# First-layer chunks beside the attention: six tiles of 256 tokens become four of 384, with the instruction order planned anew

## The chip, the cores and the metric

The kernel runs on one core of a Trainium2 chip. The metric is device time in microseconds (us) for one execution. All work is in fp32: a matrix product is either a full fp32 product or three products of rounded parts in fp32r ("high times high, high times low, low times high").

## What is computed

Causal attention over 4 batches of 8 heads, 576 positions and head width 64 (2304 tokens in all), then a gated feed-forward layer on the RMS-normalised result, then a second feed-forward layer.

```python
scores = q @ k.T / 8 + min(-(cum[i] - cum[j]), 0), causal    # cum = cumsum(max(s, 0))
x = softmax(scores) @ v                                      # heads side by side: 2304 x 512
xn = x / sqrt(mean(x * x) + 1e-6) * rms_g
x = (silu(xn @ w_gate) * (xn @ w_val)) @ w_out               # 512 -> 1536 -> 512
h = x @ w_in                                                 # 512 -> 2048
out = (h * sigmoid(1.702 * h)) @ w_out2                      # 2048 -> 512
```

## The kernel before

The program has two stages on TensorE. The first, some 250 us, is the attention, head after head; the second is a chain of products for the two feed-forward layers (`tmul`, with `chain=True`), which keeps a fixed order among its own instructions.

A head goes through these steps. `prep` loads its queries and keys. Heads 0 to 13 (`QF`) multiply in full fp32 and read the loaded tiles (slot s3, `QS` and `KS`, shown as `s_0_136`, and `KX`/`QX` in slot sc). Heads 14 to 31 are split: the pair of heads is loaded into the same slot s3, rounded and subtracted, and 12 copies from SBUF to SBUF lay the parts out as `QA`, `KA` (slot s2) and `QB`, `KB` (slot s1); their score products are fp32r. Where the first stage turns from the one form to the other, the split heads can be loaded only when the last full fp32 scores have read slot s3. I call this place the handover. `scores` is followed on VectorE by the row minimum, on ScalarE by `expo`, on GpSimd by `norm`; `transp` transposes the weights on TensorE (bank 2 and 3, copied out by ScalarE or VectorE), and for two heads together `pv` multiplies them with the values in two pieces. After 8 heads a batch is whole: `rms` sums squares on TensorE, twelve small VectorE instructions take the root, two short groups of transposes spread it (`ident,small` in the rows; bank 4, shown as `b_70`), and VectorE scales the batch's columns of `xT`, first 320 of them, then 256.

The gated layer is cut into twelve chunks of 128 of its 1536 columns. The first two (`G0`) are computed for tokens 0 to 1535 already in the first stage, beside the attention, in `fa_tile`: `TIN` cuts these tokens into tiles. I call this work the filler. Each tile is split into rounded parts (`XH`, slot sc, `sc` in the rows), multiplied with gate and value weights (`gv`: 3 matmuls to a planner's unit, 8 units to a chunk), passed through tanh and two VectorE products (`TH`, slot se), split again (`FH`, slot sd, `sd` in the rows) and multiplied with the output weights (`outp`); the product is copied to `YO` and written to DRAM (`y_d`). Before the change gate and value of a tile share bank 6 (`b_72`), 256 columns each, and the output products use bank 7 (`b_73`).

Slots are pieces of SBUF that one set of tiles after another uses. Slot sd holds `FH` until the filler ends and then `B21`, a block of the chain's left operand, so `B21` is written only after the last output product of the filler.

The order of all instructions is made by a planner in the kernel: `op` records each instruction with an estimated cost, `plan` lists them by readiness and due time, and the program then holds every engine to that order. Costs and due times are numbers in `PRM`: `HD` (due times of head pairs), `FD` (start and end of the due times of a tile's filler), `WD` (weights), `TA` (where the chain's ideal times begin), `PVC` (cost of the two pieces of `pv`), `INNER` (a factor on the cost of copies inside SBUF). A unit, recorded by one call of `op`, is never split by the planner.

Of the kernel before, what the change touches and what calls it, by code (L numbers as in the profile page):

```python
# [15 lines left out]
AF = mybir.ActivationFunctionType  # L16
ALU = mybir.AluOpType
# [7 lines left out]
PRM = {  # L25
    "G0": 2, "NWS": 18, "NWO": 6,
    "QF": set(range(14)),
    "TIN": [(t * 256, 256) for t in range(6)],
    "PPB": 5, "PTB": 12, "XHB": 7, "HHB": 5,
    "VIRT": 311296,  # L30
    "SLOTS": {
# [5 lines left out]
    },  # L37
# [8 lines left out]
    "TA": 260.97, "REB": 3, "EARLY": False, "MAG": "AV", "PASS": 0, "ISSUE": 0.6, "INNER": 1.5, "IDLE": 3, "PEN": {}, "PVC": (1.0, 2.25),  # L46
}


# [1 line left out]
def attention_then_swiglu_then_gelu(ctx: ExitStack, tc, qT, kT, vp, s, w1, w2, gT, out):  # L51
# [3 lines left out]
    P = 128  # L55
    KT = DM // P
# [3 lines left out]
    G0 = PRM["G0"]  # L60
    QF = PRM["QF"]
    TIN = PRM["TIN"]
    TS = max(n for _, n in TIN)
    TA = sum(n for _, n in TIN)
# [16 lines left out]
    PB = [pq.tile([P, 512], F32, tag=f"b{i}", name=f"b{i}") for i in range(8)]  # L81
# [17 lines left out]
    def few(n):  # L99
# [7 lines left out]

    SHAPE = {
        "Q": [S], "K": [S], "mask": [S], "SQ": [S], "VS": [5, 2 * D], "SR": [S], "ZR": [S], "CH": [S], "CL": [S], "PA": [1920], "PT": [512],
        "XH": [2, TS], "TH": [TS], "FH": [2, TS], "YO": [2, TS], "w": [2, 512], "wb": [512], "ws": [512],  # L110
        "MK": [2, 2, H2], "HH": [2, H2], "M5": [H2], "SG": [H2], "V1": [H2], "RE": [H2], **{nm: [2, 2, H2] for nm in NAMES},
    }
    ROUND = ("CH", "CL", "QA", "QB", "KA", "KB", "XH", "FH", "w", "HH", *NAMES)
# [45 lines left out]
    def get(name, n=None):  # L159
        if n is None:  # L160
            return BUF[name][0]
        return [BUF[f"{name}{i}"][0] for i in range(n)]

    QS, KS, QB, KB, QA, KA, VS, TH = (get(x, 2) for x in ("QS", "KS", "QB", "KB", "QA", "KA", "VS", "TH"))
    def wide(name, n):
        t = get(name)
        return virtual[:, t.offset:t.offset + n * S]

    mask, SQ, SQT, YO = (get(x) for x in ("mask", "SQ", "SQT", "YO"))
    PA = get("PA", NB)  # L170
    XH, FH = get("XH", PRM["XHB"]), get("FH", PRM["HHB"])
    PT = get("PT", PRM["PTB"])
# [200 lines left out]
    def tt(o_, x, y, o, eng="VG", **kw):  # L373
        op(eng, lambda e: e.tensor_tensor(out=o_, in0=x, in1=y, op=o), **kw)
# [16 lines left out]
    def dma(o_, i_, eng="S", **kw):  # L391
        op(eng, lambda e: e.dma_start(out=o_, in_=i_), dma=True, **kw)
# [38 lines left out]
    def mm3(e, o, w, wc, x, first, last):  # L431
        for n, (i, j) in enumerate(((0, 0), (0, 1), (1, 0))):
            e.matmul(o, w[:, i, wc:wc + P], x(j), start=first and n == 0, stop=last and n == 2)
# [1 line left out]


    hd = {}
    pt_i, xh_i, fh_i, th_i = [0], [0], [0], [0]

    def turn(bufs, i):  # L440
        i[0] += 1
        return bufs[(i[0] - 1) % len(bufs)]
# [92 lines left out]
    def scores(h, u):  # L535
        ps = bank(h, "s", 5 * h + u)
        blks = {0: [(1, 0, 0, 192), (0, 192, 0, 64)], 1: [(2, 0, 0, 320)], 2: [(3, 0, 0, 448)],
                3: [(4, 0, 0, 288)], 4: [(4, 0, 288, 288)]}[u]
        i = h % 2

        def fn(e):
            for qb, c0, k0, n in blks:
                q0 = Q0[qb]
                o = ps[:, c0:c0 + n]
                if h in QF:
                    kt, qt = kq_of(h)
                    e.matmul(o, qt[0:HB + 64, q0:q0 + P], kt[0:HB + 64, k0:k0 + n], start=True, stop=True)
                else:
                    e.matmul(o, QA[i][:, q0:q0 + P], KA[i][:, k0:k0 + n], start=True, stop=False)
                    e.matmul(o, QB[i][:, q0:q0 + P], KB[i][:, k0:k0 + n], start=False, stop=True)  # L550

        first_score.append(op("T", fn)["i"])
        mx = MX[h % NB]
        for qb, c0, k0, n in blks:
            pt = p_of(h, qb)
            moff = S - QK[qb] + k0 if qb else S - P
            col = 5 if k0 else qb

            def fn(e, qb=qb, c0=c0, k0=k0, n=n, pt=pt, moff=moff, col=col):
                e.tensor_tensor_reduce(  # L560
                    out=pt[:, k0:k0 + n], in0=ps[:, c0:c0 + n], in1=mask[:, moff:moff + n],
                    scale=-0.125, scalar=mx[:, 4:5] if k0 else BIG, op0=ALU.add, op1=ALU.min,
                    accum_out=mx[:, col:col + 1])

            op("V", fn)
            if qb != 4 or k0:
                expo(h, qb)
# [146 lines left out]
    def fa_tile(j, due):  # L714
        t0, n = TIN[j]
        xh = []
        for k in range(KT):
            x = xT[:, k, t0:t0 + n]
            t = turn(XH, xh_i)
            rnd("AV", t[:, 0, :n], x)  # L720
            sub(t[:, 1, :n], x, t[:, 0, :n])
            xh.append(t)
        hs = []
        steps = []

        def gv(c, u, k):
            if u == 0 and k == 0:
                fs["g"] = fs.get("g", -1) + 1
            ps = PB[PRM["BANK"]["g"][fs["g"] % len(PRM["BANK"]["g"])]].rearrange("p (u n) -> p u n", u=2)
            op("T", lambda e: mm3(e, ps[:, u, :n], WS[3 * c + u], k * P, lambda i: xh[k][:, i, :n], k == 0, k == KT - 1),  # L730
               **due())
            if u == 1 and k == KT - 1:
                th = turn(TH, th_i)[:, :n]
                hh = turn(FH, fh_i)
                hs.append(hh)
                g, v = ps[:, 0, :n], ps[:, 1, :n]
                op("A", lambda e: e.activation(out=th, in_=g, func=AF.Tanh, scale=0.5))
                op("V", lambda e: e.scalar_tensor_tensor(out=th, in0=th, scalar=1.0, in1=g, op0=ALU.add, op1=ALU.mult))
                tt(th, th, v, ALU.mult, eng="V")
                rnd("AG", hh[:, 0, :n], th)  # L740
                sub(hh[:, 1, :n], th, hh[:, 0, :n])

        def outp(c, o):
            half, i = divmod(o, 2)
            ps = PB[PRM["BANK"]["o"][0]].rearrange("p (u n) -> p u n", u=2)
            hh, w = hs[c], WS[3 * c + 2]

            def fn(e):
                for q, (x, y) in enumerate(((0, 0), (0, 1), (1, 0))):
                    e.matmul(ps[:, i, :n], w[:, x, o * P:o * P + P], hh[:, y, :n],  # L750
                             start=c == 0 and q == 0 and i == 0, stop=c == G0 - 1 and q == 2 and i == 1)

            op("T", fn, **due())
            if c == G0 - 1 and i == 1:
                def cpy(e):
                    if e.tag == "A":
                        e.activation(out=YO[:, :, :n], in_=ps[:, :, :n], func=AF.Copy, scale=0.5)
                    else:
                        e.tensor_scalar(out=YO[:, :, :n], in0=ps[:, :, :n], scalar1=0.5, scalar2=1.0, op0=ALU.mult, op1=ALU.mult)

                op("AV", cpy)
                dma(y_d[:, 2 * half:2 * half + 2, t0:t0 + n], YO[:, :, :n])

        for c in range(G0):
            for u in range(2):
                for k in range(KT):
                    gv(c, u, k)
            if c:
                for o in range(2):
                    outp(c - 1, o)  # L770
        for o in range(2):
            outp(G0 - 1, o)
        for c in range(G0):
            for o in (2, 3):
                outp(c, o)

    fill_n = [0]
    per = G0 * (2 * KT + KT)

    def fill_due():  # L780
        j, i = divmod(fill_n[0], per)
# [690 lines left out]
```

## Time and profile before

| | us |
|---|---|
| median of 3 runs (1001.4 to 1001.81) | 1001.64 |
| the profiled execution | 1002.01 |
| its span, first to last instruction | 1000.2 |
| TensorE busy in that span | 990.4 |
| VectorE, ScalarE, GpSimd busy | 655.0, 563.0, 286.1 |

The span is what the trace covers; 1.8 us of the profiled execution lie around it. A matmul counts as busy from its start to the modelled end of its pipeline, so that neighbours overlap; how long TensorE needs for one of a row of equal matmuls is read from the distance between starts instead.

### The profile page before, as it was taken

The page shows a single profiled execution, that of the slowest core. Times are in us where ns is not written, and L with a number is a line of the kernel's source. Part 1 is how long each engine was busy: PE and PEld are TensorE (multiplying, and loading weights), DVE is VectorE, ACT ScalarE, POOL GpSimd, SP SyncE. Part 2 cuts the span into 40 slices and gives each one's busy share as a digit, 9 for nine tenths or more (in the row PEclk, how much of TensorE's full clock was granted, in tenths as well). Part 3 has the DMA queues.
Part 4 walks back from the last instruction along what each step waited for, and adds up shares of the span by engine and source line. Part 5 has one row for each costly group of instructions (what it writes and reads, how often), then busy time and mean ns, then how long its engine had stood idle before and what let it go on. Part 6 is the DMA issues. An engine that isn't in the chain of part 4 may idle for free.

```text
span 1000.2 us, 16551 instructions
## 1 busy us (share of the span) xinstructions
PE 990.4 (99%) x5882; PEld 910.7 (91%) x5882; DVE 655.0 (65%) x1532; ACT 563.0 (56%) x1298; POOL 286.1 (29%) x388
## 2 busy tenths in 40 slices
PE   9999999999999999999999999999999999999998
PEld 6777888898999999999999999999889998899987
DVE  8777886777878888546766858874653564353323
ACT  8988786786576555334544436776644463353322
POOL 5666653554332133102322303332320231020000
PEclk9999999999999999999999999999999999999999
DMA  5247766853775762661583676653375045505541
GB/s 181 91 126 183 211 176 177 205 140 118 278 256 225 281 240 98 242 221 43 170 317 144 241 287 231 273 205 123 108 281 221 29 161 232 189 1 197 207 165 63
DMA packets 63050, 183.51 MB, mean 183 GB/s; under 512 B 7028, under 2 KB 23924, under 8 KB 62968
## 3 DMA queue, kind: packets, MB, share of 16 engines
q1 hardware_dynamic: 62968, 182.46, 53.1%
q8 instruction: 46, 0.75, 0.3%
q14 instruction: 36, 0.29, 0.1%
HBM read 122.32 MB, written 44.19 MB: 166 GB/s over the span
## 4 chain that ended last, share of the span: by engine, by line
PE 89%; DVE 4%; ACT 2%; DMA 2%; issue 1%; SPq 1%; POOL 0%; DVEq 0%; ACTq 0%
PE b L208 89%; DVE s L208 1%; ACT s L208 1%; DVE xT L208 1%; SPq L208 1%; DMA s<-in_kT_dram 1%; DMA s<-in_qT_dram 1%; DMA y_d<-sc 0%; DVE b L208 0%; DVE sf L208 0%; POOL wa L208 0%; DVE sc L208 0%; DMA s<-s 0%; ACT st L208 0%; ACT si L208 0%
## 5 line engine op out<-in xcount | busy, mean ns | idle before, releaser
L208 ACT ACTIVATE s<-b 128x384 f32<-128x384 f32 (+1 forms) x267 | 127.6, 489 | 146.4 <-PE b L208 81.2
L208 DVE TENSOR_TENSOR xT<-b,xT 128x384 f32<-128x384 f32 (+1 forms) x158 | 92.6, 599 | 88.7 <-PE b L208 88.0
L208 ACT ACTIVATE b<-b 128x384 f32<-128x384 f32 x125 | 58.2, 478 | 107.8 <-DVE b L208 72.0
L208 POOL TENSOR_TENSOR wa<-wa,st 128x512 int32<-128x512 int32 x50 | 65.9, 1319 | 171.7 <-DVE wa L208 79.0
L208 DVE TENSOR_TENSOR s<-b,s 128x384 fp32r<-128x384 f32 (+1 forms) x121 | 66.4, 553 | 67.3 <-ACT s L208 62.7
L208 PE MATMUL b<-s,w 128*128 128x384 f32 x540 | 107.4, 336 | 0.5 <-DVE s L208 0.3
L208 PE MATMUL b<-s 128*128 128x288 f32 (+11 forms) x420 | 99.2, 361 | 1.8 <-DVE small L208 1.4
L208 PEld LDWEIGHTS b<-s,w 128*128 128x128 f32 x540 | 94.9, 188 | 2.1 <-DVE s L208 1.4
L208 POOL TENSOR_SCALAR wm<-wm 128x512 f32<-128x512 f32 x68 | 41.8, 615 | 140.4 <-ACT wm L208 41.9
L208 PEld LDWEIGHTS b<-s 128*128 128x128 f32 (+1 forms) x420 | 66.9, 192 | 14.8 <-issue 6.3
L208 DVE TENSOR_TENSOR b<-b,s 128x384 f32<-128x384 f32 x82 | 46.1, 562 | 51.6 <-PE b L208 41.4
L208 PE MATMUL b<-sc,w 128*128 128x256 f32 (+1 forms) x396 | 67.3, 304 | 0.0
L208 POOL TENSOR_SCALAR s<-s,small 128x192 f32<-128x192 f32 (+4 forms) x100 | 52.2, 542 | 33.1 <-DVE small L208 11.9
L208 ACT ACTIVATE s<-s,small 128x448 f32<-128x448 f32 (+4 forms) x100 | 55.1, 551 | 9.8 <-DVE small L208 9.6
L208 ACT ACTIVATE st<-st 128x512 int32<-128x512 uint32 x68 | 45.6, 673 | 22.3 <-DMA st<-in_w_dram 22.1
L208 PEld LDWEIGHTS b<-sc,w 128*128 128x128 f32 x396 | 57.1, 189 | 1.0 <-DVE se L208 0.2
L208 PE MATMUL b<-sd,w 128*128 128x384 f32 (+1 forms) x312 | 56.3, 313 | 0.3 <-ACT se L208 0.3
L208 PE MATMUL b<-s,s 128*128 128x384 f32 (+1 forms) x252 | 54.9, 346 | 0.0
L208 PE MATMUL b<-w,s 128*128 128x512 f32 x189 | 51.1, 391 | 0.0
L208 PE MATMUL b<-s,sk 128*128 128x384 f32 x246 | 50.8, 335 | 0.2 <-DVE s L208 0.2
L208 DVE CUSTOM_DVE_ANT_0 s<-b,s 128x288 f32<-128x288 f32 (+4 forms) x100 | 39.3, 424 | 15.7 <-PE b L208 15.5
L208 PEld LDWEIGHTS b<-sd,w 128*128 128x128 f32 x312 | 49.1, 189 | 0.5 <-ACT se L208 0.5
(267 smaller groups left out, 2390.6 us busy)
## 6 DMA issues: line engine op xcount, KB each, us to landing
st<-in_w_dram SPq DMA_DIRECT2D x68, 512.0 KB
s<-s SPq DMA_DIRECT2D x108, 144.0 KB
xT<-y_d SPq DMA_DIRECT2D x3, 1536.0 KB
s<-pc11B SPq DMA_DIRECT2D x6, 768.0 KB
s<-pc21B SPq DMA_DIRECT2D x6, 768.0 KB
out_dram<-xT SPq DMA_DIRECT2D x18, 256.0 KB
s<-in_vp_dram SPq DMA_DIRECT2D x16, 256.0 KB
y_d<-se SPq DMA_DIRECT2D x12, 256.0 KB
```

Of the source, the lines that this page charges most:

```text
L208: return lambda *args, **kw: f(*[real(x) for x in args], **{k: real(x) for k, x in kw.items()})
```

## The change

The filler's tiles are 384 tokens wide, four in place of six, over the same 1536 tokens. A tile's gate has bank 6 to itself and its value bank 7. The tanh of a chunk and the first VectorE product are recorded behind the last gate unit instead of behind the last value unit. An output product of both chunks is one unit of 6 matmuls (before: two units of 3, in banks shared by two outputs); the four of a tile alternate between banks 6 and 7, each is copied out alone (128x384 in place of 128x512), and each is written to DRAM by a DMA of its own, 16 DMAs in place of 12. There are four `XH` buffers for the four of a tile (before 7), three of `FH` (5), one `TH` (2), and two of `YO`. The scores of each head get due times (`SD`), all other due times are new, `TA` goes from 260.97 to 257.35, `INNER` from 1.5 to 1.0, and `PVC` from (1.0, 2.25) to (0.81, 2.22). So the planner puts out another order, in the first stage above all.

```diff
-    "TIN": [(t * 256, 256) for t in range(6)],
-    "PPB": 5, "PTB": 12, "XHB": 7, "HHB": 5,
+    "TIN": [(t * 384, 384) for t in range(4)],
+    "PPB": 5, "PTB": 12, "XHB": 4, "HHB": 3,
...
-    "TA": 260.97, "REB": 3, "EARLY": False, "MAG": "AV", "PASS": 0, "ISSUE": 0.6, "INNER": 1.5, "IDLE": 3, "PEN": {}, "PVC": (1.0, 2.25),
+    "TA": 257.35, "REB": 3, "EARLY": False, "MAG": "AV", "PASS": 0, "ISSUE": 0.6, "INNER": 1.0, "IDLE": 3, "PEN": {}, "PVC": (0.81, 2.22),
...
-        first_score.append(op("T", fn)["i"])
+        sd = PRM["SD"][h]
+        first_score.append(op("T", fn, due=sd if sd < 690 else None, g=f"s{h}")["i"])
...
         def gv(c, u, k):
-            if u == 0 and k == 0:
-                fs["g"] = fs.get("g", -1) + 1
-            ps = PB[PRM["BANK"]["g"][fs["g"] % len(PRM["BANK"]["g"])]].rearrange("p (u n) -> p u n", u=2)
-            op("T", lambda e: mm3(e, ps[:, u, :n], WS[3 * c + u], k * P, lambda i: xh[k][:, i, :n], k == 0, k == KT - 1),
+            ps = PB[PRM["BANK"]["go"[u]][0]]
+            op("T", lambda e: mm3(e, ps[:, :n], WS[3 * c + u], k * P, lambda i: xh[k][:, i, :n], k == 0, k == KT - 1),
                **due())
+            if u == 0 and k == KT - 1:
+                fs["th"] = turn(TH, th_i)[:, :n]
+                th = fs["th"]
+                op("A", lambda e: e.activation(out=th, in_=ps[:, :n], func=AF.Tanh, scale=0.5))
+                op("V", lambda e: e.scalar_tensor_tensor(out=th, in0=th, scalar=1.0, in1=ps[:, :n], op0=ALU.add, op1=ALU.mult))
...
-        def outp(c, o):
-            half, i = divmod(o, 2)
-            ps = PB[PRM["BANK"]["o"][0]].rearrange("p (u n) -> p u n", u=2)
-            hh, w = hs[c], WS[3 * c + 2]
+        def outp(o):
+            ps = PB[PRM["BANK"]["go"[o % 2]][0]][:, :n]
 
             def fn(e):
-                for q, (x, y) in enumerate(((0, 0), (0, 1), (1, 0))):
-                    e.matmul(ps[:, i, :n], w[:, x, o * P:o * P + P], hh[:, y, :n],
-                             start=c == 0 and q == 0 and i == 0, stop=c == G0 - 1 and q == 2 and i == 1)
+                for c in range(G0):
+                    for q, (x, y) in enumerate(((0, 0), (0, 1), (1, 0))):
+                        e.matmul(ps, WS[3 * c + 2][:, x, o * P:o * P + P], hs[c][:, y, :n],
+                                 start=c == 0 and q == 0, stop=c == G0 - 1 and q == 2)
...
-    per = G0 * (2 * KT + KT)
+    per = G0 * 2 * KT + KT
```

Over the whole program TensorE gets 288 filler matmuls of 384 columns for 432 of 256 columns; nothing else is taken off it or added to it. In the order before these 432 stand in 59 runs between other work, in the new order the 288 stand in 39.

The first place is TensorE's order at the handover (`s_0_136`: full fp32 scores; `s_0_885` and `s_0_231`, now `s_0_928` and `s_0_234`: the tiles of split heads; `64x...` rows: `pv`). Between the last full fp32 score and the first split one stand, before, 41 transposes, two groups of three for the root, and one first piece of `pv`. These are the last rows of it:

```order
L208 MATMUL b_69<-ident,s_0_159 128x128 x3
L208 MATMUL b_68<-ident,s_0_165 128x128 x4
L208 MATMUL b_69<-ident,s_0_165 128x128 x4
L208 MATMUL b_70<-sb_397,s_0_149 64x256
L208 MATMUL b_70<-sf_289,s_0_149 64x256
L208 MATMUL b_70<-sb_397,s_0_149 64x128
L208 MATMUL b_70<-sf_289,s_0_149 64x128
L208 MATMUL b_67<-s_0_885 128x192
```

And now:

```order
L211 MATMUL b_68<-ident,s_0_165 128x128 x4
L211 MATMUL b_72<-sc_915,w_125 128x384 x3
L211 MATMUL b_69<-ident,s_0_165 128x128 x4
L211 MATMUL b_68<-ident,s_0_165 128x128 x4
L211 MATMUL b_72<-sc_915,w_125 128x384 x3
L211 MATMUL b_70<-sg_309,s_0_149 64x256
L211 MATMUL b_70<-sb_377,s_0_149 64x256
L211 MATMUL b_70<-sg_309,s_0_149 64x128
L211 MATMUL b_70<-sb_377,s_0_149 64x128
L211 MATMUL b_69<-ident,s_0_165 128x128 x3
L211 MATMUL b_68<-ident,s_0_131 128x128 x4
L211 MATMUL b_67<-s_0_928 128x192
```

What moved: the groups for the root went ahead of the last full fp32 score, a first and a second piece of `pv` came in behind it, and six filler matmuls with one more first piece stand ahead of the split score. In all the stretch now holds 37 transposes, two first pieces and one second piece of `pv`, and 6 filler matmuls.

The second place is TensorE's order where the filler ends and the chain takes over (`sd_1363`, now `sd_1339`: the filler's output products; `sd_3073`, now `sd_2903`: block `B21`; `sg` and `sf`: blocks of the last batch's tokens). Before:

```order
L208 MATMUL b_70<-ident,small 128x64
L208 MATMUL b_73<-sd_1363,w_127 128x256 x6
L208 MATMUL b_73<-sd_1363,w_130 128x256 x6
L208 MATMUL b_70<-ident,small 128x64
L208 MATMUL b_70<-ident,small 128x128
L208 MATMUL b_70<-ident,small 128x64
L208 MATMUL b_66<-sd_3073,sl_2871 128x384 x6
L208 MATMUL b_67<-sd_3073,sk_2763 128x384 x6
L208 MATMUL b_68<-s_1_2773,sl_2871 128x384 x6
```

And now:

```order
L211 MATMUL b_73<-sd_1339,w_130 128x384 x3
L211 MATMUL b_70<-ident,small 128x128 x2
L211 MATMUL b_70<-ident,small 128x64
L211 MATMUL b_66<-sd_2903,sl_2676 128x384 x6
L211 MATMUL b_67<-sd_2903,sk_2623 128x384 x6
L211 MATMUL b_68<-s_1_2532,sl_2676 128x384 x6
L211 MATMUL b_70<-ident,small 128x64
L211 MATMUL b_70<-ident,small 128x128
L211 MATMUL b_70<-ident,small 128x64
L211 MATMUL b_69<-s_1_2532,sk_2623 128x384 x6
```

What moved: the first group for the root came behind the last output product, and the second went 18 matmuls down the chain. From the second group to the first `sg` row there are 36 matmuls before and 18 now.

The third place is VectorE at the same point, from the first scaling of the last batch to the low part of `sf`. Before:

```order
L208 SCALAR_TENSOR_TENSOR xT<-xT,small,b_70 128x320 x4
L208 TENSOR_TENSOR s_1_2735<-xT,s_1_2735 128x768
L208 TENSOR_TENSOR sd_3073<-xT,sd_3073 128x768
L208 SCALAR_TENSOR_TENSOR xT<-xT,small,b_70 128x256 x4
L208 TENSOR_TENSOR wm<-wa,s_1_2920 128x256
L208 TENSOR_TENSOR sg_3094<-xT,sg_3094 128x768
L208 TENSOR_TENSOR b_67<-s_1_3104,b_67 128x384
L208 TENSOR_TENSOR sf_3107<-xT,sf_3107 128x768
```

And now:

```order
L211 TENSOR_TENSOR sd_2903<-xT,sd_2903 128x768
L211 SCALAR_TENSOR_TENSOR xT<-xT,small,b_70 128x320 x3
L211 TENSOR_TENSOR s_1_2526<-xT,s_1_2526 128x768
L211 TENSOR_SCALAR se_1179<-b_73 128x384
L211 TENSOR_TENSOR b_67<-s_1_2928,b_67 128x384
L211 TENSOR_SCALAR wm<-st_121 128x512
L211 TENSOR_TENSOR sd_2903<-xT,sd_2903 128x768
L211 SCALAR_TENSOR_TENSOR xT<-xT,small,b_70 128x256 x4
L211 TENSOR_TENSOR s_1_2757<-b_67,s_1_2757 128x384
L211 TENSOR_TENSOR sg_2966<-xT,sg_2966 128x768
L211 TENSOR_TENSOR b_69<-s_1_2928,b_69 128x384
L211 TENSOR_TENSOR sf_2978<-xT,sf_2978 128x768
```

What moved: five instructions more stand between the first scaling (one 128x320 row of it is ahead of the rows shown) and the low part of `sf`: a copy out of bank 7, the second writing of slot sd, a step of weight decoding, one low part and one sum of the chain's hidden values.

## Rows read from the trace of the kernel before

**Rows 1.** The page: busy time of an engine, share of the span, instructions.

```profile
PE 990.4 (99%) x5882; PEld 910.7 (91%) x5882; DVE 655.0 (65%) x1532; ACT 563.0 (56%) x1298; POOL 286.1 (29%) x388
```

**Rows 2.** Windows: stretch, length, busy us (instructions) of PE, PEld, DVE, ACT, POOL; granted clock; DMA.

```profile
0.00:20.00 20.00, 18.56 (x72) 12.50 (x73) 15.63 (x64) 16.18 (x47) 10.64 (x36) 1.00 0.65 200
...
100.00:150.00 50.00, 49.44 (x415) 43.98 (x415) 41.54 (x150) 39.24 (x118) 28.80 (x45) 1.00 0.73 194
...
250.00:265.00 15.00, 14.17 (x81) 13.30 (x80) 14.06 (x23) 12.26 (x20) 2.67 (x4) 1.00 0.75 288
...
400.00:600.00 200.00, 200.00 (x1156) 200.00 (x1155) 127.14 (x247) 85.07 (x174) 38.78 (x41) 1.00 0.56 208
```

**Rows 3.** Timeline of TensorE around filler runs: start, length, instruction, count.

```profile
95.84 0.96 PE L208 MATMUL b<-sc,w 128*128 128x256 f32 x6
96.64 1.03 PE L208 MATMUL b<-ident,si 128*128 128x128 f32 x8
97.43 0.60 PE L208 MATMUL b<-sc,w 128*128 128x256 f32 x3
...
118.94 0.52 PE L208 MATMUL b<-sc,w 128*128 128x256 f32 x3
119.30 0.72 PE L208 MATMUL b<-s 128*128 128x320 f32 x4
...
124.27 2.68 PE L208 MATMUL b<-sc,w 128*128 128x256 f32 x21
126.78 0.58 PE L208 MATMUL b<-ident,small 128*128 128x128 f32 x3
```

**Rows 4.** Timeline of TensorE at the handover; in brackets idle time and what ended it.

```profile
72.71 2.44 PE L208 MATMUL b<-s 96*128 96x192 f32 x10
74.98 0.49 PE L208 MATMUL b<-ident,si 128*128 128x128 f32 x3
...
83.23 0.43 PE L208 MATMUL b<-sb,s 128*64 128x256 f32 x1
...
84.41 0.62 PE L208 MATMUL b<-s 128*128 128x192 f32 x4 [0.32 <-DMA s<-s]
84.96 0.38 PE L208 MATMUL b<-sb,s 128*64 128x192 f32 x1
...
87.17 1.22 PE L208 MATMUL b<-s 128*128 128x448 f32 x6
```

**Rows 5.** The chain that ended last, at the handover: start, length, what.

```profile
81.67 2.50 DMA s<-s
```

**Rows 6.** Waits of TensorE over the span: total, times, longest.

```profile
PE b L208 <- DMA s<-s: 0.3, 1, 0.3
```

**Rows 7.** Timeline of TensorE where the filler ends.

```profile
251.16 0.72 PE L208 MATMUL b<-ident,small 64*128 64x64 f32 x3
252.15 0.44 PE L208 MATMUL b<-sd,sl 128*128 128x384 f32 x1 [0.28 <-ACT sd L208]
253.14 1.14 PE L208 MATMUL b<-sd,sl 128*128 128x384 f32 x5 [0.55 <-DVE sd L208]
...
259.32 2.24 PE L208 MATMUL b<-sg,w 128*128 128x384 f32 x12
```

**Rows 8.** Timeline of VectorE at the same place.

```profile
249.18 1.92 DVE L208 SCALAR_TENSOR_TENSOR xT<-xT,small,b 128x320 f32<-128x320 f32 x4
251.09 1.03 DVE L208 TENSOR_TENSOR s<-xT,s 128x768 fp32r<-128x768 f32 x1
252.13 0.96 DVE L208 TENSOR_TENSOR sd<-xT,sd 128x768 fp32r<-128x768 f32 x1
253.01 1.65 DVE L208 SCALAR_TENSOR_TENSOR xT<-xT,small,b 128x256 f32<-128x256 f32 x4
...
254.91 0.95 DVE L208 TENSOR_TENSOR sg<-xT,sg 128x768 fp32r<-128x768 f32 x1
256.59 0.56 DVE L208 TENSOR_TENSOR b<-s,b 128x384 f32<-128x384 f32 x1 [0.73 <-ACT s L208]
```

More of the change, by code (lines that the diff above doesn't have):

```diff
@@ L109, in attention_then_swiglu_then_gelu @@
         "Q": [S], "K": [S], "mask": [S], "SQ": [S], "VS": [5, 2 * D], "SR": [S], "ZR": [S], "CH": [S], "CL": [S], "PA": [1920], "PT": [512],
-        "XH": [2, TS], "TH": [TS], "FH": [2, TS], "YO": [2, TS], "w": [2, 512], "wb": [512], "ws": [512],
+        "XH": [2, TS], "TH": [TS], "FH": [2, TS], "YO": [TS], "w": [2, 512], "wb": [512], "ws": [512],
         "MK": [2, 2, H2], "HH": [2, H2], "M5": [H2], "SG": [H2], "V1": [H2], "RE": [H2], **{nm: [2, 2, H2] for nm in NAMES},
@@ L162, in get @@
         return [BUF[f"{name}{i}"][0] for i in range(n)]
-    QS, KS, QB, KB, QA, KA, VS, TH = (get(x, 2) for x in ("QS", "KS", "QB", "KB", "QA", "KA", "VS", "TH"))
+    QS, KS, QB, KB, QA, KA, VS = (get(x, 2) for x in ("QS", "KS", "QB", "KB", "QA", "KA", "VS"))
+    TH = get("TH", 1)
     def wide(name, n):
@@ L167, in wide @@
         return virtual[:, t.offset:t.offset + n * S]
-    mask, SQ, SQT, YO = (get(x) for x in ("mask", "SQ", "SQT", "YO"))
+    mask, SQ, SQT = (get(x) for x in ("mask", "SQ", "SQT"))
+    YO = get("YO", 2)
     PA = get("PA", NB)
@@ L437, in attention_then_swiglu_then_gelu @@
     hd = {}
-    pt_i, xh_i, fh_i, th_i = [0], [0], [0], [0]
+    pt_i, xh_i, fh_i, th_i, yo_i = [0], [0], [0], [0], [0]
     def turn(bufs, i):
@@ L731, in gv @@
                **due())
+            if u == 0 and k == KT - 1:
[3 more added lines that the diff above has]
+                op("V", lambda e: e.scalar_tensor_tensor(out=th, in0=th, scalar=1.0, in1=ps[:, :n], op0=ALU.add, op1=ALU.mult))
             if u == 1 and k == KT - 1:
-                th = turn(TH, th_i)[:, :n]
+                th = fs["th"]
                 hh = turn(FH, fh_i)
@@ L735, in gv @@
                 hs.append(hh)
[L736 to L739, printed above, removed]
+                tt(th, th, ps[:, :n], ALU.mult, eng="V")
                 rnd("AG", hh[:, 0, :n], th)
                 sub(hh[:, 1, :n], th, hh[:, 0, :n])
-        def outp(c, o):
-            half, i = divmod(o, 2)
-            ps = PB[PRM["BANK"]["o"][0]].rearrange("p (u n) -> p u n", u=2)
-            hh, w = hs[c], WS[3 * c + 2]
+        def outp(o):
+            ps = PB[PRM["BANK"]["go"[o % 2]][0]][:, :n]
@@ L753, in outp @@
             op("T", fn, **due())
[L754 to L762, printed above, removed]
+            yo = turn(YO, yo_i)[:, :n]
@@ L764, in fa_tile, with cpy @@
+            def cpy(e):
+                if e.tag == "A":
+                    e.activation(out=yo, in_=ps, func=AF.Copy, scale=0.5)
+                else:
+                    e.tensor_scalar(out=yo, in0=ps, scalar1=0.5, scalar2=1.0, op0=ALU.mult, op1=ALU.mult)
+            op("AV", cpy)
+            dma(y_d[:, o, t0:t0 + n], yo)
         for c in range(G0):
@@ L767, in fa_tile @@
                     gv(c, u, k)
[L768 to L775, printed above, removed]
+        for o in range(KT):
+            outp(o)
     fill_n = [0]
-    per = G0 * (2 * KT + KT)
+    per = G0 * 2 * KT + KT
     def fill_due():
```

11 rows, old and new, of the table PRM are left out of this document.

## The prediction

> **What bounds the kernel now.** I read the page first: TensorE is busy for 990.4 of 1000.2 us and no other engine for more than 655 [rows 1]. A matmul's busy time runs to the modelled end of its pipeline, so 99% alone says little; the windows say more. From 400 to 600 us the chain runs 1156 matmuls in 200.00 us, one every 173.0 ns, with nothing between them [rows 2]. There TensorE's own work sets the time, VectorE is busy for 127 of 200 us and GpSimd for 39, and a chain that begins earlier ends earlier by as much. So the change is worth what it takes off the first stage, the 250 us ahead of the chain. In that stage TensorE still shows 49.44 of 50 us busy from 100 to 150 us, while VectorE has 41.5 and ScalarE 39.2 [rows 2]: TensorE bounds it too, but not everywhere. At the handover it has too little to do, since split heads wait for their copies, and from 250 to 265 us VectorE is busy for 14.06 of 15 us [rows 2] and TensorE waits for it.
>
> The profiled execution, 1002.01 us, is 0.37 us above the median of the runs, 1001.64. The sum is made against the former, and 0.37 us is taken off at the end.
>
> **The change part by part.**
>
> *A, wider matmuls.* 21 filler matmuls of 256 columns that follow each other take 126.78 - 124.27 = 2.51 us, 119.5 ns each [rows 3]. The chain's 384 columns take 173.0 ns [rows 2]. The 128 columns between them cost 53.5 ns, 0.418 ns each, which is one column per cycle of 2.4 GHz, the level granted throughout (1.00 in rows 2); so each matmul has 12.5 ns that its width doesn't change. Before: 432 x 119.5 = 51.6 us. Now: 288 x 173.0 = 49.8 us. Saved: 1.8 us, or the 144 matmuls fewer at 12.5 ns. Both prices are measured here on the same engine, weights and types, so I give it only 0.2 us to either side.
>
> The Trainium skill (TensorE: Matmul & The Clock Gate, section "Back-to-back issue gap") gives the distance of two matmuls as columns over 2.4 plus 2.5 ns: 109 and 162.5 ns, so A would be 144 x 2.5 ns = 0.4 us and the forecast below 1.4 us later, about 1000. The trace's distances are longer than the page's by 10 ns at both widths; the rows are used.
>
> *B, fewer runs of filler.* 59 runs between attention work become 39. A run of six took 96.64 - 95.84 = 0.80 us, 0.08 more than 6 x 119.5 ns; a run of three took 119.30 - 118.94 = 0.36 us, no more than 3 x 119.5 [rows 3]. So a run costs 0 to 0.08 us in changing over; I take 0.04, the middle, since both kinds occur side by side. 20 runs fewer give 0.8 us (0 to 1.6).
>
> *C, the handover.* The last full fp32 scores end and the next transposes start at 74.98 us; the first split score starts at 84.41, behind a wait for a copy [rows 4], and the chain that ended last runs through that copy, 2.50 us from issue to landing [rows 5]. What TensorE had to do in these 9.43 us: 41 transposes at 0.099 (eight took 97.43 - 96.64 [rows 3]), 4.1 us; two groups for the root, some 0.6 each (0.72 with its pipeline's end [rows 7]); one first piece of `pv`, 84.41 - 0.32 - 83.23 = 0.86 [rows 4]. In all 6.2 us, so 3.2 were lost. The new order puts 37 transposes (3.7), two first pieces (1.7), one second piece (87.17 - 84.96 = 2.2 [rows 4]) and six filler matmuls (1.0) there: 8.6 us, or 2.4 more. If loading, splitting and copying take as long as before, 2.4 us of idle time are filled with work that stood elsewhere. If something ahead, on ScalarE above all, makes the last full fp32 heads later too, nothing is gained. I take 1.8 us of the 0 to 2.4, since three of the four kinds moved there need only data of older heads.
>
> *D, where the filler ends.* Slot sd turns into `B21` only behind the last output product; TensorE waited 0.28 us for ScalarE's high part and then 0.55 for VectorE's low part [rows 7]. That wait stays: in the new order, too, `sd` products follow the filler with only three transposes between. But now these three are the first group for the root, and VectorE's scaling starts only behind them. From 251.16 to the first `sg` product at 259.32 are 8.16 us [rows 7], of which 36 x 0.173 + 0.5 = 6.7 are work: 1.4 lost. In the new order TensorE has 36 x 0.173 + 1.0 = 7.2 us from the first group to `sg`. VectorE has, up to `sg`'s low part, 1.92 + 0.96 + 1.03 + 1.65 + 0.95 as before [rows 8], and besides a second `sd` (0.96), two instructions on 384 columns of PSUM (0.56 each), and a copy and a decoding step that I price at the same 0.56: 9.7 us. So `sg` starts some 2.4 us behind TensorE's own work where it was 1.4: 1.0 us lost (0 if the pipelines overlap as well as before, 2.5 with two more waits for ScalarE such as the 0.73 in rows 8).
>
> *E, copies for split heads.* The planner now takes a copy's transfer for a third shorter (`INNER`), and SP issues 16 output DMAs in place of 12 in the queue that holds the copies. TensorE waited once, 0.3 us, for a copy [rows 6]. If the new order leaves less room, it waits more often: 18 split heads at 0 to 0.3 us each are 0 to 5.4 us. I take 0.5, near the one wait seen, since most copies had room to spare.
>
> *Without a price of their own:* 32 fewer filler instructions on VectorE, ScalarE and GpSimd (a tile has 22, before 20, but four tiles stand for six), with the same elements; hidden, since none of them bounds the stretch from 100 to 250 us, and at 0.06 to 0.1 us each at most 3 us on engines that had 8 to 20 us to spare in every 50 [rows 2]. The single `TH` and separate banks: tanh can now run while the value fills its own bank; twelve matmuls of 173 ns (2.1 us) lie between the filling of a bank and its next filling, and the two instructions that free it (one on ScalarE, one on VectorE, 0.56 us for 384 columns [rows 8]) fit in, so no wait. What else the new order does between 20 and 250 us I can't price from the order; TensorE shows 0.56 us idle in 50 from 100 on [rows 2], so I put nought, 1.5 us to either side.
>
> Sum: -1.8 - 0.8 - 1.8 + 1.0 + 0.5 = -2.9 us. 1002.01 - 2.9 = 999.1 for a profiled execution, 998.7 for the median.
>
> **The rivals.** A measurement of this kernel can tell about 0.2%, 2 us, from no change.
>
> *Only the columns count.* The filler multiplies the same 1536 tokens, and the handover is set by ScalarE and the copies whatever TensorE does meanwhile: A stays, B and C are nil, D and E cost 1.5. That gives -0.3, 1001.3, no difference. For it speaks that the chain that ended last runs through a copy there [rows 5]; against it, that the new order has other work at that place. The page's smaller price for A would bring the sum to -1.5, also no difference.
>
> *VectorE holds the chain's start.* D costs 2.5 us and B nothing: -1.8 + 2.5 - 1.8 + 0.5 = -0.6, 1001.0. VectorE's 14.06 of 15 us [rows 2] speak for it; that its chain had 3.4 us to spare for `sg` (low part done at 255.86, used from 259.32) speaks against it.
>
> *Copies come late: slower.* Order and queue are fixed, so a score that waits for its copy holds everything behind it on TensorE. At 0.45 us for each of 18 heads E is 8.1 us in place of 0.5, and the sum +4.7: 1006.3. It turns slower than before by over 0.2% from 0.3 us a head. For it: the lower price in the planner, and a copy's 2.50 us [rows 5]. Against it: one wait of 0.3 us in the whole trace [rows 6].
>
> **How the numbers follow.** The forecast holds with 0.55 (of that 0.5 faster by over 0.2%, below 999.6), only the columns count 0.17, VectorE holds the start 0.10, copies come late 0.10, and 0.08 for a gain larger than forecast, in order I can't price (faster). Faster 0.58, within 0.2% 0.32, slower 0.10. Range: the gains at their ends (1.8 + 1.6 + 2.4) without D and E are 5.8 us, 995.8; the other way, the two cases of no difference reach 1001.3, and with 1 us for the unpriced order 1002.2. Outside this lie the late copies and little else.
>
> **What would show it.** A: 288 filler matmuls 173 ns apart. B: 39 runs with 0 to 0.08 us over. C: the first split score some 2 us earlier relative to the work before it; TensorE's idle time between the last full fp32 score and it down from 3.2 us to about 1. D: a wait for VectorE before the first `sg` product that wasn't there. E: waits of TensorE for `s<-s` DMAs of less than 1 us in total. I am wrong if the first `sg` product starts no earlier than 258 us (259.32 before [rows 7]), if those DMA waits add up to 5 us, or if the chain itself, closed before, shows gaps because decoded weights come late.

## The result and the profile after

The changed kernel takes 1007.42 us in the median of 6 runs (1005.75 to 1010.78), the kernel before 1001.72 (1001.37 to 1002.0). The ratio is 1.006 [1.0048, 1.0072]: slower by 5.7 us, where 998.7 was forecast and the range ended at 1002.2. The profiled execution took 1007.22 us, its span is 1005.4 (1000.2 before). The page, answering to [rows 1]:

```profile
PE 990.2 (98%) x5738; PEld 907.1 (90%) x5738; DVE 657.4 (65%) x1524; ACT 562.5 (56%) x1292; POOL 272.2 (27%) x370
```

TensorE is as busy as before, with 144 matmuls fewer and 5.2 us more of span. Where the time lies is seen in windows of the first stage, here of the kernel after (columns as in [rows 2]):

```profile
20.00:118.00 98.00, 97.34 (x719) 76.37 (x718) 76.92 (x288) 86.27 (x251) 56.19 (x96) 1.00 0.54 145
118.00:247.00 129.00, 123.04 (x916) 106.27 (x915) 99.04 (x316) 95.06 (x264) 56.33 (x95) 1.00 0.62 161
247.00:270.00 23.00, 20.81 (x115) 19.03 (x115) 20.61 (x48) 14.03 (x24) 3.29 (x4) 1.00 0.64 238
270.00:320.00 50.00, 49.34 (x283) 48.65 (x283) 36.95 (x70) 28.29 (x57) 18.44 (x17) 1.00 0.74 258
```

and of the kernel before:

```profile
20.00:118.00 98.00, 95.91 (x716) 74.04 (x715) 76.07 (x283) 82.82 (x244) 65.79 (x107) 1.00 0.52 145
118.00:247.00 129.00, 128.44 (x1078) 115.42 (x1078) 97.69 (x341) 98.72 (x277) 59.16 (x99) 1.00 0.62 163
247.00:270.00 23.00, 21.60 (x124) 20.10 (x124) 21.85 (x38) 13.98 (x23) 8.00 (x9) 1.00 0.74 279
270.00:320.00 50.00, 49.85 (x286) 49.16 (x285) 37.30 (x68) 31.15 (x63) 15.21 (x16) 1.00 0.69 245
```

Length less PE's busy time is TensorE's idle time. Up to 118 us, with the handover in it, it falls from 2.09 to 0.66 us: 1.43 won. From 118 to 247 us it rises from 0.56 to 5.96 us: 5.40 lost. Where the filler ends it rises from 1.40 to 2.19, and behind that from 0.15 to 0.66. What TensorE waited for between 118 and 247 us, after (in us, times, longest; two smaller waits, of 0.3 and 0.2, follow):

```profile
PE b L211 <- POOL s L211: 1.4, 2, 1.3
PE b L211 <- DMA s<-ch_d: 1.4, 1, 1.4
PE b L211 <- DVE small L211: 0.8, 3, 0.4
PE b L211 <- POOL si L211: 0.7, 1, 0.7
PE b L211 <- DVE xT L211: 0.5, 1, 0.5
PE b L211 <- DMA s<-s: 0.4, 2, 0.2
```

The same view of before has one row:

```profile
PE b L208 <- ACT xT L208: 0.6, 1, 0.6
```

So there is no one new wait: normalised weights from GpSimd, copies, VectorE's scale factors, each late one to three times. The largest, on TensorE:

```profile
167.19 0.77 PE L211 MATMUL b<-sc,w 128*128 128x384 f32 x3
167.80 0.25 PE L211 MATMUL b<-s 128*128 128x192 f32 x1
169.49 1.28 PE L211 MATMUL b<-s 128*128 128x192 f32 x7 [1.43 <-DMA s<-ch_d]
```

and SP's queue ahead of it:

```profile
155.30 7.01 SPq L211 DMA_DIRECT2D s<-s  x10
162.41 0.54 SPq L211 DMA_DIRECT2D s<-in_qT_dram  x1
...
165.18 0.44 SPq L211 DMA_DIRECT2D s<-ch_d  x1
165.72 1.05 SPq L211 DMA_DIRECT2D s<-in_vp_dram  x2
166.86 0.39 SPq L211 DMA_DIRECT2D s<-ch_d  x1
```

SP issues without a pause from 155.30 to 167.25 us, and what the score needs stands behind input loads. By the trace's semaphores the matmul waited for two transfers: a copy `s<-s` issued at 164.12, which landed at 169.22, and the first of the two loads from `ch_d` (4.5 KB each, out of DRAM), issued at 165.18 and landed at 169.35. That is 5.1 and 4.2 us, where [rows 5] has 2.50 for a copy, and TensorE has stood still for 1.43. The DMA engines are busy for 0.85 of the time and more from 162 to 168 us, so the place in the queue need not be the only reason.

### The profile page after: what moved, and what is told of

Its sections match the earlier page's. It is cut to its first block, busy times and chain, and to the rows that moved or that the text cites. A ratio compares the mean times of both kernels' runs of the same rounds, so it can differ in the third digit from the quotient of the medians.

```text
span 1005.4 us, 16237 instructions
## 1 busy us (share of the span) xinstructions
PE 990.2 (98%) x5738; PEld 907.1 (90%) x5738; DVE 657.4 (65%) x1524; ACT 562.5 (56%) x1292; POOL 272.2 (27%) x370
## 5 line engine op out<-in xcount | busy, mean ns | idle before, releaser
L211 ACT ACTIVATE s<-s,small 128x576 f32<-128x576 f32 (+4 forms) x100 | 55.2, 554 | 13.7 <-DVE small L211 13.1
L211 POOL TENSOR_SCALAR s<-s,small 128x448 f32<-128x448 f32 (+4 forms) x100 | 51.6, 535 | 38.9 <-DVE wm L211 13.9
L211 PE MATMUL b<-sc,w 128*128 128x384 f32 x300 | 61.3, 341 | 0.0
L211 PE MATMUL b<-sd,w 128*128 128x384 f32 x264 | 52.4, 336 | 0.0
L211 PEld LDWEIGHTS b<-sc,w 128*128 128x128 f32 x300 | 51.4, 188 | 0.3
L211 PE MATMUL b<-s,sc 128*128 128x384 f32 x228 | 47.2, 334 | 0.0
```

The lines of the kernel that those rows point to most:

```text
L211: return lambda *args, **kw: f(*[real(x) for x in args], **{k: real(x) for k, x in kw.items()})
```

## The experiments

The forecast's own explanation for a slower kernel was late copies. Three theories were set against each other first: T1, the planner's lowered prices (`INNER`, `PVC`) pack copies and `pv` too tightly; T2, the wide tiles and long units themselves lose; T3, the due times do. "Theory 4", named later, is that no number is wrong by itself and the order as a whole came out badly.

**Old prices in the new kernel.**

```diff
-"INNER": 1.0
+"INNER": 1.5
-"PVC": (0.81, 2.22)
+"PVC": (1.0, 2.25)
```

> The changed kernel with the planner's two costs set back (INNER 1.5, PVC 1.0 and 2.25), so that it plans anew; all else as changed. Theory 1, the lowered costs make the planner pack copies and pv too tightly, and TensorE's waits between 118 and 247 us come from that: 998 to 1000.5 us, and under 2 us of TensorE waits there (6.4 in the changed kernel). Theory 2, the wide tiles and long units themselves leave too little to fill with: 1004 us or more. Theory 3, the due times (SD, HD, FD) put the heads in a bad order: 1004 us or more, with waits at the same heads.

1002.68 us (1001.2 to 1004.38), ratio to before 1.0015 [1.0006, 1.0024]. 4.7 us of the loss go away with two numbers that change nothing but the planner's decisions.

**New prices in the old kernel** (the same edit the other way in the kernel before).

> The kernel before with nothing but the planner's two costs lowered as in the change. Theory 1: slower than before by 3 us or more, 1005 us, with new waits of TensorE after 120 us. Theories 2 and 3: 1000.5 to 1002.5 us, no difference.

1003.88 us (1002.97 to 1006.66), 1.003 [1.0018, 1.0043]: some 2.8 us slower. Both go the way of T1, though neither by its figures: it had 998 to 1000.5 for the first, and 3 us or more for the second.

**The new filler code on old numbers**: prices, `TA`, `HD` and `WD` of before and `SD` all 700, once with six tiles of 256 (and `FD` of before), once with four of 384 (`FD` of the change). The edit of the first:

```diff
-    "TIN": [(t * 384, 384) for t in range(4)],
+    "TIN": [(t * 256, 256) for t in range(6)],
-"TA": 257.35
+"TA": 260.97
...
-    "SD": [331.83, 393.3, 216.64,
+    "SD": [700.0] * 32,
```

> The new filler code (gate and value in a bank each, output product in units of 6, tanh behind the gate) on six tiles of 256 tokens, with all of the planner's numbers as before and no due times for scores. It keeps 432 matmuls. Theory 1 and theory 3: 1000 to 1003 us, about as before. Theory 2, as far as the long units and not the width are its cause: 1004 us or more.

1008.9 us (1006.78 to 1009.96), 1.0069 [1.0057, 1.0082].

> Four tiles of 384 tokens with the new filler code, but the planner's costs and HD, WD and TA as before, no due times for scores; FD has to stay as changed (a pair for each tile). Theory 1 and theory 3: 998 to 1000.5 us, since 1.8 us of matmul time are saved and the heads are planned as before. Theory 2: 1004 us or more.

1009.93 us (1009.38 to 1010.23), 1.0084 [1.0071, 1.0098]. Neither T1 nor T3 allows these times: old prices and old due times, and slower than the change. T2 does, and stands until the same operations are run in a better order, below. Each has its longest wait in a place of its own. The 256 tiles wait once for GpSimd:

```profile
233.36 1.97 PE L211 MATMUL b<-ident,s 128*128 128x128 f32 x8 [3.51 <-POOL s L211]
```

and the 384 tiles in the chain, between 270 and 320 us:

```profile
PE b L211 <- ACT s L211: 2.9, 1, 2.9
```

In both, TensorE's granted clock falls from 2.4 to 1.2 GHz behind these waits and again behind those where the filler ends. It stays there for 10.2 us in all with the 256 tiles and for 6.8 with the 384, so 5.1 and 3.4 us of these times are the clock's.

**One price at a time, and the due times of the scores alone.** In the changed kernel the copy's price only:

```diff
-"INNER": 1.0
+"INNER": 1.5
```

> The changed kernel with one planner price put back: a copy's transfer (INNER) 1.5 in place of 1.0; the price of a pv group (PVC) stays lowered. Putting back both gave 1002.7 us against 1007.4 for the changed kernel. Theory 1a (the copies are planned too short, so transposes and scores that need them are placed too early): nearly all of that returns here, 1002 to 1003.5 us, and TensorE's waits between 118 and 247 us fall from about 6 us to 3 or less. Theory 1b (pv is planned too short, so everything that ScalarE, VectorE and GpSimd must do beside it is planned too densely): 1006 to 1007.5 us. Rival 4 (no price is wrong by itself; every change of a number shuffles the whole order, and an order comes out well or badly by luck): a time outside both bounds, or above 1007.5 us.

1000.48 us (998.94 to 1001.73), 0.9991 [0.9982, 1.0].

In the changed kernel the other price only:

```diff
-"PVC": (0.81, 2.22)
+"PVC": (1.0, 2.25)
```

> The changed kernel with the other price put back: PVC (1.0, 2.25) in place of (0.81, 2.22); the copy's price stays lowered. Theory 1a: 1006 to 1007.5 us. Theory 1b: 1002 to 1003.5 us. If both prices count, this run and the one with the old copy price together give back about 4.7 us, some 2 us each, 1005 us. Rival 4: outside of these.

1002.0 us (1000.97 to 1003.0), 1.0006 [0.9997, 1.0015].

In the kernel before the copy's price only:

```diff
-"INNER": 1.5
+"INNER": 1.0
```

> The kernel before with one number of the change: the copy's price 1.0 in place of 1.5, PVC as before. With both prices lowered the kernel before took 1003.9 us, 2.8 more than its own 1001.1. Theory 1a: 1003 to 1004.5 us. Theory 1b: 1001 us, no difference. Rival 4: faster than 1000 or slower than 1005.

1000.49 us (999.55 to 1002.71), 0.9995 [0.9987, 1.0004].

In the changed kernel no due times for scores:

```diff
-    "SD": [331.83, 393.3, 216.64,
+    "SD": [700.0] * 32,
```

> The changed kernel without the new due times of the scores (SD all at 700, which leaves the scores unforced); both prices stay lowered. Theory 3 (the due times set the bad order): 1001 to 1004 us. Theory 1 (the lowered prices do): 1006 to 1008.5 us, with TensorE's waits between 118 and 247 us at 5 us or more. Rival 4: outside of both.

1001.13 us (999.77 to 1004.57), 1.0001 [0.9992, 1.0011]. With this T1 falls as it stood: each of three repairs alone gives back 5.4 to 6.9 us, more than both prices together, and the low copy price does the kernel before no harm. T3 had 1001 to 1004 us for the last of them, and that is what came; but it had allowed the prices no gain. What they have in common is that the operations stay and the order changes.

**Copies ahead in SP's queue, all other orders kept.** This tests the copies themselves.

```diff
+    for o in ops:
+        if o["byts"] and (o["inner"] or o["byts"] < 5000) and start[o["i"]] > 100.0:
+            start[o["i"]] = max([start[o["i"]] - 4.0] + [finish[d] + 0.001 for d in o["deps"]])
```

> The changed kernel, order kept on TensorE, ScalarE, VectorE and GpSimd; only in SP's own order the copies between on-chip tiles (and the small ones of the decay rows) stand up to 4 us earlier from 100 us on, ahead of input loads and output transfers, as far as the work that writes their source allows (48 places change, by at most 4 places). Theory E (the loss is scores that wait behind SP's queue for late copies: 1.43 us at 169.49, 2.5 us of weight loads in all): 1003 to 1005 us, and TensorE's waits for DMAs between 118 and 247 us fall from 2.5 us to under 0.8. Theory 4 (the loss is spread over many small waits for all engines in one unlucky order): 1006 to 1008 us, DMA waits replaced by others.

1009.95 us (1006.01 to 1011.88), 1.0079 [1.0064, 1.0094]: no gain, and the wait for a copy moved and grew:

```profile
149.82 0.41 PE L211 MATMUL b<-s 128*128 128x192 f32 x1 [2.78 <-DMA s<-s]
```

SP takes its queue in order, so bringing some copies forward puts others back. Late copies are one form that a bad order takes; moving them by rule doesn't cure it. The windows behind that wait show what made it dear; the figure ahead of the DMA columns is the granted clock:

```profile
148.00:150.00 2.00, 0.18 (x1) 0.20 (x1) 0.08 (x1) 0.67 (x2) 1.75 (x4) 0.98 0.84 180
150.00:152.00 2.00, 1.69 (x6) 1.41 (x6) 0.51 (x4) 0.17 (x1) 0.81 (x2) 0.50 0.97 224
...
154.00:156.00 2.00, 2.00 (x11) 1.98 (x10) 1.34 (x4) 1.46 (x5) 0.00 (x0) 0.50 0.53 147
156.00:158.00 2.00, 2.00 (x13) 1.92 (x13) 0.71 (x3) 1.35 (x4) 0.00 (x0) 0.82 0.52 147
158.00:160.00 2.00, 2.00 (x18) 1.92 (x17) 0.94 (x5) 1.35 (x4) 1.55 (x3) 1.00 0.59 216
```

The clock is at its lower level, 1.2 in place of 2.4 GHz, for some 6.8 us, so half of that, 3.4 us, is lost besides the wait. From 194 to 198 us it is there again, for 3.4 us, behind waits of 0.51 and 1.28 us that the changed kernel has too; that is another 1.7 us. Together the 5.1 us are about what this profiled execution, 1011.88 us, took longer than the changed kernel's, 1007.22, in which the clock didn't fall. The one run here with a mean clock of 0.999 took 1006.01 us. So by themselves the moved copies changed little either way.

**Two small steps from the change**, each by itself:

```diff
-"INNER": 1.0
+"INNER": 1.1
...
-"TA": 257.35
+"TA": 257.85
```

> The changed kernel with INNER 1.1 in place of 1.0: a tenth more for a copy, next to no change in what the price says. If the price itself matters (too low: bad; 1.5: good), 1.1 stays near the changed kernel: 1006 to 1008 us. Theory 4 (any number reshuffles the order, and the changed kernel's order is one of the poorer draws): the time can be anywhere in the scatter of the orders tried, 1000 to 1005 us more likely than 1007.

1007.38 us (1006.4 to 1007.67), 1.006 [1.0048, 1.0072]. The total is that of the changed kernel, and what was expected if the price itself matters; the place isn't. TensorE is idle for 1.33 us from 118 to 247 us, and the first `sf` product starts at 258.5, 8 us earlier; then the chain itself stops:

```profile
282.70 0.44 PE L211 MATMUL b<-s,w 128*128 128x384 f32 x1 [3.35 <-ACT s L211]
```

```profile
280.00:290.00 10.00, 6.52 (x20) 6.27 (x21) 9.23 (x18) 7.70 (x15) 0.61 (x1) 0.66 0.87 328
```

Behind that wait the clock is at the lower level for 6.8 us, 3.4 us of loss.

> The changed kernel with the planned start of the chain, TA, at 257.85 in place of 257.35; no price and no other due time changes. If prices or the due times of scores are at fault: 1006 to 1008 us. Theory 4: in the scatter, 1000 to 1005 us more likely than 1007.

1005.39 us (1003.21 to 1009.89), 1.0048 [1.003, 1.0065]; the waits lie where the changed kernel has them, for the most part. Theory 4 in its bare form, that any number throws the dice anew, had 1000 to 1005 as likelier than 1007 for both and misses: both stay bad, one at a new place.

**An order found anew for the same operations.**

```diff
-    "HD": [16.92, 309.44, 401.69,
...
+    "HD": [565.29, 257.91, 565.44, 404.07, 364.45, 3.33, 80.12, 128.11, 357.16, 443.02, 583.15, 332.16, 612.86, 106.16, 338.4, 90.25],
+    "FD": [(0.0, 175.21), (20.98, 335.08), (181.0, 80.09), (53.41, 586.77)],
+    "WD": [280.74, 160.24, 450.68, 347.36, 453.23, 688.38],
+    "SD": [254.22, 700.0, 299.94, 526.3, 17.15, 673.64, 475.46, 650.35, 349.94, 700.0, 700.0, 365.52, 310.79, 139.45, 446.44, 722.77, 433.37, 151.02, 689.07, 700.0, 708.14, 441.3, 704.09, 700.0, 700.0, 133.61, 330.71, 685.04, 745.35, 403.26, 531.41, 777.36],
-"TA": 257.35, "INNER": 1.0, "PVC": (0.81, 2.22)
+"TA": 212.34, "INNER": 1.79, "PVC": (0.78, 2.25)
```

The numbers were chosen so that the planned order also holds up when handovers between engines, and copies, take longer than the planner prices them.

> The changed kernel's operations, unchanged, in another order: due times of heads, filler, weights and scores, TA and the two prices (INNER 1.79, PVC (0.78, 2.25)) set anew, chosen so that the order also holds where handovers between engines and copies take longer than the planner says. If the tile width and longer units (A, C) are worth what they were worked out to be and only the order spoilt them: faster than before, 996 to 999.5 us. If four tiles of 384 lose by themselves (two banks that both product and output use, tail at the chain's start): not under 1000 us.

994.53 us (993.74 to 995.19), 0.9932 [0.992, 0.9944]: 6.8 us faster than before and 12.9 faster than the change, from the change's own operations. With this T2 falls too. (The planner also decides which engine takes an operation that several can: VectorE has 1524 instructions in the changed kernel and 1509 here, GpSimd 370 and 383. "Order" includes that choice.) The windows:

```profile
118.00:247.00 129.00, 127.93 (x959) 113.24 (x960) 99.52 (x332) 98.09 (x272) 62.39 (x100) 1.00 0.64 175
247.00:270.00 23.00, 23.00 (x132) 22.41 (x131) 20.62 (x37) 14.78 (x25) 10.96 (x11) 1.00 0.65 248
```

TensorE is idle for 1.07 us from 118 to 247 us, and not at all from 247 to 270, where the change idled for 2.19. The waits for `B21` stay, ahead of that window, but `sg` follows without the 0.27 and 0.79 us that it cost in the changed kernel:

```profile
246.28 1.14 PE L211 MATMUL b<-sd,sl 128*128 128x384 f32 x5 [0.55 <-DVE sd L211]
...
253.33 2.24 PE L211 MATMUL b<-sg,w 128*128 128x384 f32 x12
```

**Controls.** First the operations of the kernel before, six tiles of 256, with due times for scores and an order found in the same way:

```diff
-    "FD": [(81.45, 266.42), (370.15, 642.27), (623.02, 333.64), (53.78, 479.65), (120.6, 622.93), (183.91, 170.5)],
+    "FD": [(354.7, 256.58), (142.24, 268.81), (25.27, 630.48), (486.77, 305.81), (490.8, 165.56), (487.93, 306.6)],
...
-"TA": 260.97, "INNER": 1.5, "PVC": (1.0, 2.25)
+"TA": 168.3, "INNER": 1.75, "PVC": (0.81, 2.19)
```

> The control to the searched order of the changed kernel (994.5 us): the operations of the kernel before (six tiles of 256, gate and value in one bank), with due times for the scores added and all due times, TA and the two prices (INNER 1.75, PVC (0.81, 2.19)) set anew by the same means and with as much effort. If the gain comes from the order alone: 994 to 996 us, as with 384. If the tiles are worth what A and B say (1.8 + 0.8 us) beside the order: 996.5 to 998.5 us. If the four wide tiles are worth nothing and 994.5 was a lucky order: under 994.

996.05 us (995.93 to 997.44), 0.9955 [0.9943, 0.9968]. Then a second order of this kind for the four tiles of 384, from other due times throughout:

```diff
-"TA": 257.35, "INNER": 1.0, "PVC": (0.81, 2.22)
+"TA": 229.11, "INNER": 1.77, "PVC": (0.78, 2.19)
```

> A second, separately found order for the changed kernel's operations (other due times throughout, INNER 1.77, PVC (0.78, 2.19)). If such orders hold on the chip by what they have in common (room ahead of each handover and copy): 994 to 997 us. If 994.5 was luck: anywhere from 995 to 1003.

995.31 us (994.45 to 995.47), 0.994 [0.9926, 0.9954]. So three orders found this way are all good, and 5 us of the 6.8 come without the tiles. The tiles add 1.5 or 0.7 us (996.05 - 994.53, 996.05 - 995.31); the second isn't clear of noise, since the ratios' intervals overlap, and two orders for the same tiles differ by 0.8.

The searched due times (994.53 us) with the change's prices:

```diff
-"INNER": 1.79, "PVC": (0.78, 2.25)
+"INNER": 1.0, "PVC": (0.81, 2.22)
```

> The searched order's due times (994.5 us) with the changed kernel's prices, INNER 1.0 and PVC (0.81, 2.22). If the low copy price makes an order bad: slower by 4 us or more, 998.5 to 1005 us. If due times and prices only have to fit each other, any change of one without the other shuffles the order: also slower, by 2 to 8 us; same (994 to 995.5 us) only if the price doesn't matter.

999.67 us (998.67 to 1003.05), 0.9993 [0.9983, 1.0003].

The change's due times with the searched prices:

```diff
-"INNER": 1.0, "PVC": (0.81, 2.22)
+"INNER": 1.79, "PVC": (0.78, 2.25)
```

> The changed kernel's due times with the prices of the searched order, INNER 1.79 and PVC (0.78, 2.25). If the price is what makes the searched order good: 994 to 999 us, and TensorE's waits between 118 and 247 us fall under 2 us. If the due times and the prices have to be found together: 999 to 1006 us (with INNER 1.5 alone put back it was 1000.5).

1003.29 us (1002.34 to 1004.84), 1.0022 [1.0013, 1.0031]. Low prices spoil good due times by 5.1 us, and the searched prices mend the change's due times by 4.1, less than `INNER` 1.5 alone did (6.9): no price is good by itself, and the best time here needs both halves as they were found.

## Why the prediction was wrong

**The step that failed** is the last of the change's parts: "What else the new order does between 20 and 250 us I can't price from the order; [...] so I put nought, 1.5 us to either side." In the profiled execution it was worth 5.4 us by TensorE's idle time between 118 and 247 us. By the waits of its weight loads in that window, which also count where the preceding matmul's modelled end covers a gap, it is more: the rows other than "issue" add to 10.3 us against 1.9. The largest of them after (the first holds the wait for the copy named above):

```profile
PEld b L211 <- DMA s<-s: 2.5, 3, 1.6
PEld b L211 <- POOL s L211: 1.7, 2, 1.4
```

The bound of 1.5 us came from how little TensorE idled before, 0.56 us in 50 [rows 2]. That row says how good the old order was, and nothing of a new one; and the range took only 1 us of the 1.5. The orders of one set of operations, the changed kernel's, spread from 994.5 to 1010.0 us here. A change that plans the order anew had to be given that scatter.

**A** was right. Eighteen filler matmuls take 117.94 - 114.81 = 3.13 us, 173.9 ns each:

```profile
114.81 3.29 PE L211 MATMUL b<-sc,w 128*128 128x384 f32 x18
117.94 0.58 PE L211 MATMUL b<-ident,small 128*128 128x128 f32 x3
```

The estimate of 162.5 ns by the Trainium skill (TensorE: Matmul & The Clock Gate, "Back-to-back issue gap"), whose formula the page gives for an isolated matmul and not for a stream with weight loads, isn't borne out: the trace has 173.9, as it had 173.0 before.

**B** was near: 1.1 us saved, 0.8 forecast. The price of a run was taken from two samples, and the middle, 0.04 us, is too low. A run of three takes 167.80 - 167.19 = 0.61 us in the rows above, where 3 x 173 is 0.52. Over all runs with no wait in them, the time above 119.5 ns a matmul is 4.1 us in the 57 of before, and that above 173.0 ns is 3.0 us in the 37 of now: 0.07 and 0.08 us a run. Between the searched orders A and B are seen as 1.5 or 0.7 us, against the 2.6 reckoned. There the runs don't fall from 59 to 39 but to 45 and 46, and these cost 4.7 and 4.1 us against 4.8, so B is worth 0.1 or 0.6; A's 1.8 is within what two orders differ by.

**C** was right in kind. Between the last full fp32 scores and the first split score:

```profile
78.31 0.75 PE L211 MATMUL b<-s 96*128 96x288 f32 x2
78.90 0.49 PE L211 MATMUL b<-ident,sk 128*128 128x128 f32 x3
...
88.56 0.98 PE L211 MATMUL b<-s 128*128 128x192 f32 x6
```

88.56 - 78.90 = 9.66 us for 8.6 us of work, 1.1 lost where it was 3.2. The windows up to 118 us show 1.43 us less idle time, against 1.8 forecast.

**D** was right in kind and size. From the first group for the root to the first `sg` product are 263.32 - 253.68 = 9.64 us, 2.4 more than the 7.2 of work, as reckoned, and the low part of `sg` is waited for, as said:

```profile
253.68 0.58 PE L211 MATMUL b<-ident,small 128*128 128x128 f32 x3
254.84 0.45 PE L211 MATMUL b<-sd,sl 128*128 128x384 f32 x1 [0.57 <-ACT sd L211]
255.83 1.14 PE L211 MATMUL b<-sd,sl 128*128 128x384 f32 x5 [0.55 <-DVE sd L211]
...
263.32 0.44 PE L211 MATMUL b<-sg,w 128*128 128x384 f32 x1 [0.27 <-ACT sg L211]
264.56 2.17 PE L211 MATMUL b<-sg,w 128*128 128x384 f32 x11 [0.79 <-DVE sg L211]
```

0.8 us more idle time between 247 and 270 us, 1.0 forecast. The first `sg` product starts at 263.32, past the 258 that the text gave as the sign of being wrong.

**E** was too small. Its sign, waits of less than 1 us for `s<-s`, holds by the letter (0.4 us). But the 1.4 us put down to `ch_d` stood in the same queue, and the copy issued ahead of it landed only 0.13 us earlier. With them the waits come to 1.8 us on TensorE, 0.5 forecast, within the bounds of 0 to 5.4. The rival "copies come late" gave nearly the right time, 1006.3, by a cause that is a third of it at most. It also rested on the lowered `INNER`, which alone does the kernel before nothing (1000.49).

The sum by what was measured: A and B 2.6 us as reckoned, C 1.4 won; 5.4, 0.8 and (behind 270 us) 0.5 lost. That is +2.7, or +5.7 with the weight loads' 8.4 (10.3 - 1.9) in place of 5.4; the spans differ by 5.2. By idle time alone it closes: -1.4 + 5.4 + 0.8 + 0.5 = 5.3, while TensorE's busy time falls by only 0.2 us (990.4 to 990.2). So what A and B saved doesn't show in this order's busy time. The weight loads' waits grew by 3.0 us more than the idle time did, which would cover it; no run tells the two apart.

**What stays open**: which of the numbers made this order bad. Taking out either price or the scores' due times repairs it, and a small step of `INNER` or `TA` doesn't. That the order loses the time, and not the operations, is shown, by the same operations at 994.5 and 995.3 us.

## What to carry to other kernels

Where a change also re-plans a fixed order, forecast the order's scatter first (here 15 us, of which 3.4 to 5.1 in the slowest orders are the clock's, against the 2.6 us reckoned for the tiles), and compare the operations only under orders found with equal effort. Prices and due times that were found together are one thing: one of them put into another set cost up to 5.1 us and gave up to 6.9 here. The three orders that did well were chosen for room ahead of every handover, and the one rule tried on the changed kernel's order instead, copies up to 4 us ahead, moved the loss elsewhere. That it is the room that makes them hold is likely and not shown: no run varies it alone.

## What the runs showed of the hardware

A short wait of TensorE can cost more than its length, since the granted clock can fall behind it, from 2.4 to 1.2 GHz. With copies ahead in SP's queue a wait of 2.78 us was followed by some 6.8 us at the lower level. With the changed kernel's due times and the searched prices a wait of 1.53 us, up to 121.58 us, was followed by 3.4 us of it. With `TA` half a microsecond later two waits, together 1.82 us, were enough:

```profile
186.10 0.72 PE L211 MATMUL b<-ident,small 64*128 64x64 f32 x3 [0.54 <-DVE xT L211]
188.10 1.07 PE L211 MATMUL b<-ident,s 128*128 128x128 f32 x4 [1.28 <-POOL s L211]
```

```profile
188.00:190.00 2.00, 1.90 (x8) 1.20 (x10) 1.57 (x5) 0.79 (x2) 2.00 (x4) 0.55 0.95 245
```

It isn't the same in every execution. The changed kernel has the same two waits, of 0.51 and 1.27 us, and in the execution profiled the clock stays at 1.00 behind them, as it does behind its 1.43 us at 168 to 169.5:

```profile
188.76 0.66 PE L211 MATMUL b<-ident,s 128*128 128x128 f32 x4 [1.27 <-POOL s L211]
```

```profile
188.00:190.00 2.00, 1.24 (x12) 0.89 (x12) 2.00 (x7) 0.54 (x2) 2.00 (x5) 1.00 0.94 235
```

With `TA` half a microsecond later the times go with it: the runs with a mean clock of 1.000 took 1003.2 and 1003.9 us, those at 0.998 took 1005.0 and 1005.8, at 0.997 1008.1, and at 0.994 1009.9. It doesn't explain every spread. The changed kernel's six runs lie at 0.996 to 0.999 and spread over 5.0 us, but not in the clock's order: 1007.22 us at 0.999, 1005.75 at 0.998, 1007.63 at 0.996. With the copy's price at 1.1 all five lie at 0.996 and spread over 1.3. The searched order's five lie at 0.999 to 1.000 and spread over 1.5.
